# Retention attention and a dropless mixture of experts in one kernel: where the routing, the loads and the scaling stand in the attention steps

## The chip, the cores and the metric

The kernel runs on one core of a Trainium2 chip, in one launch. The metric is the device time of the launch in microseconds. Before the change it is 497.69 us, the median of three runs (497.06 to 498.72).

## What is computed

Four sequences of 768 tokens with 8 heads of 64 go through a recurrent retention; the result, read as 3072 rows of 512 features, goes through a mixture of 8 experts in which each row takes its best expert and no row is dropped.

```python
for t in range(S):                                       # B, H, S, D = 4, 8, 768, 64
    state = gamma * state + k[:, :, t] outer v[:, :, t]
    y[:, :, t] = scale * q[:, :, t] @ state
x = y.transpose(0, 2, 1, 3).reshape(3072, 512)
logits = x @ w_gate                                      # 512 x 8
e = argmax(logits); gate_w = softmax(logits)[e]
out = gate_w * (relu(x @ w1[e]) @ w2[e])                 # w1: 8 x 512 x 1024, w2: 8 x 1024 x 512
```

All is in float32.

## The kernel before, in words

The attention is cut into 12 steps, `steps = [(m, b)]`: three blocks m of 256 tokens for each of the four sequences b. In a step the 256 tokens lie on 128 partitions as pairs (e = 0, 1). A recurrence over 256 tokens becomes matrix products: `scale_q` and `scale_k` (L388 to L400) multiply q and k by powers of gamma, with GpSimd for all steps but the first; `transpose` (L402) turns them on TensorE into PSUM tiles `tr`, and ScalarE copies them to `qT` and `kT`; `scores` (L433) multiplies kT with qT into PSUM tiles `sc`, and VectorE masks them into `am` (L445); `values` (L473) multiplies `am` with v into y; `products` (L448) forms k-v products `new`, which VectorE adds to the running state (L466, L468); `past` (L488) adds q times the old state to y, and copies y to `xTg`, two copies for y[1]; `to_rows` (L508) transposes it to rows `xg` on VectorE, and `store` (L516) writes a group of rows to DRAM as `x_d`.

A group c is 512 rows, those of two steps, and is ready behind the second of them. `place(c)` (L531) is its routing, a generator that is advanced in pieces: `parts` (products with w_gate) and the group's store; `lgp` (transposes), logits, argmax and gate, a chain of small VectorE operations; `rk` (ranks of rows within their expert) and another chain (`seen` to `at`); the piece from `told` to `here`; and `found`, a product that puts row numbers into an inverse list `inv`. In group 3 (`FIRST`) the head of that list, `src_e`, then starts four early gathers of rows of the first expert from `x_d`, by GpSimd's indirect DMAs, into `xs2`.

The order on PE, ScalarE, GpSimd, VectorE and the DMA queue SP is the order in which the program writes the instructions (`manual_schedule`); each engine takes its instructions in turn and waits for semaphores. Before the change a step s reads: values(s), products(s), load(s+3), scaling of s+2, scores(s+1), past(s), one piece of routing, two `to_rows`, transpose(s+2), one piece of routing. Groups are chained: the next one's pieces begin where the last one's end. After step 11 the early rows are brought into order (`early_rows`, VectorE copies to `xe`, PE transposes `tre`), and the expert layers begin: `layer1` (L218, `hp`) for 256 early rows of expert 0, `pair` (L266, `yp`, a seven-product scheme for layer 2), then for every expert `layer1` and `layer2` (`ye`).

PSUM has 8 buffers here, four with the tag "sc" (for `sc`, `new`, `rk`, `found`, `hp`) and four with "ty" (for `y`, `tr`, `parts`, `lgp`, `tre`, `yp`, `ye`). A tile takes the buffer that was given up longest ago, and its first matmul waits for the last reader of the tile before.

Of the kernel before, what the change touches and what calls it, by code (L numbers as in the profile page):

```python
# [13 lines left out]
F32 = mybir.dt.float32  # L14
# [4 lines left out]
ALU = mybir.AluOpType  # L19
AX = mybir.AxisListType  # L20

P = 128


NC = 6
# [16 lines left out]
def inner(ap, n):  # L42

    dims = [list(d) for d in ap.ap]
    return bass.AP(tensor=ap.tensor, offset=ap.offset, ap=dims + [[0, n]])


def middle(ap, n):

    dims = [list(d) for d in ap.ap]  # L50
    return bass.AP(tensor=ap.tensor, offset=ap.offset, ap=[dims[0], [0, n]] + dims[1:])
# [3 lines left out]
def kernel(  # L55
# [11 lines left out]
    nc = tc.nc  # L67
    B, H, S, D = q.shape
# [3 lines left out]
    HP = H // 2  # L72
    NT = N // P
    DT = DM // P
# [14 lines left out]
    def ps(tag, bufs, name):  # L89
        return psum.tile([P, 512], F32, tag=tag, name=name, bufs=bufs)  # L90

    L = 32
    Q = P // L
# [226 lines left out]
    HALF = EARLY // P  # L320
# [26 lines left out]
    with ExitStack() as actx:  # L347
# [29 lines left out]
        def load(s):  # L377

            m, b = steps[s]
            got = {}  # L380
            for nm, src in (("k", k), ("q", q), ("v", v)) if s else (("q", q), ("k", k), ("v", v)):
                got[nm] = att.tile([P, H, 2 * D], F32, tag=nm, name=nm, bufs=2 if nm == "q" else 3)
                for hs in ([ts(i, HP) for i in range(2)] if s == 0 else [slice(0, H)]):
                    nc.sync.dma_start(got[nm][:, hs, :], src[b, hs, ts(m, 2 * P), :].rearrange(
                        "h (t e) d -> t h (e d)", e=2))
            qkv[s] = got

        def scale(s, nm, kept, base, bufs, muls):  # L388
            m, b = steps[s]
            kept[s] = att.tile([P, 2, H, D], F32, tag=f"{nm}s", name=f"{nm}s", bufs=bufs)  # L390
            for hs in ([ts(i, HP) for i in range(2)] if s == 0 and nm == "q" else [slice(0, H)]):
                for e in range(2):
                    muls[e].tensor_tensor(out=kept[s][:, e, hs, :], in0=qkv[s][nm][:, hs, ts(e, D)],  # L393
                                          in1=inner(dec[:, ts(base + 2 * m + e, H)][:, hs], D), op=ALU.mult)

        def scale_q(s, muls=[nc.gpsimd] * 2):
            scale(s, "q", qss, 0, 2, muls)

        def scale_k(s, muls=[nc.gpsimd] * 2):
            scale(s, "k", kss, NC, 3, muls)  # L400

        def transpose(s):  # L402


            of = {"q": qss.pop(s), "k": kss[s]}
            kT = att.tile([P, HP, 2, P], F32, tag="kT", name="kT", bufs=1)
            qT = att.tile([P, HP, P, 2], F32, tag="qT", name="qT")

            def turned(nm, es, pieces=1):
                trs = [ps("ty", 4, "tr").rearrange("p (a t) -> p a t", a=HP) for _ in es]  # L410
                for i in range(pieces):
                    for e, tr in zip(es, trs):
                        for a in range(i * HP // pieces, (i + 1) * HP // pieces):
                            nc.tensor.transpose(
                                tr[:, a, :], of[nm][:, e, 2 * a : 2 * a + 2, :].rearrange("p h d -> p (h d)"), ident)
                return trs

            def q_turned():
                for e, tr in enumerate(turned("q", range(2), 2) if s == 0 else [turned("q", [e])[0] for e in range(2)]):
                    (nc.vector.tensor_copy if e and s == 0 else nc.scalar.copy)(qT[:, :, :, e], tr)  # L420

            if s == 0:
                q_turned()
            for e in range(2):
                nc.scalar.copy(out=kT[:, :, e, :], in_=turned("k", [e])[0])  # L425
            if s:
                q_turned()
            front[s] = (kT, qT)
# [102 lines left out]
        def place(c):  # L531
# [14 lines left out]
            for b in range(B):  # L546
                nc.tensor.transpose(tr[:, b, :], lgT[:, ts(b, P)], ident)  # L547
            lg = att.tile([P, B, E], F32, tag="lg", name="lg")
# [26 lines left out]
            nc.tensor.matmul(rk, lhsT=ones_b, rhs=middle(acc[:, c, :], B), start=False, stop=True)  # L575
            seen = att.tile([P, E], F32, tag="seen", name="seen")
# [17 lines left out]
            if c < NC - 1:  # L594
                yield
# [32 lines left out]
        AHEAD = 3  # L628
# [3 lines left out]
        scale_q(0, [nc.vector] * 2)  # L632
        scale_k(0, [nc.gpsimd, nc.vector])
        transpose(0)
        nc.sync.dma_start(wg[:, :, 0:E], w_gate.rearrange("(dt p) e -> p dt e", p=P))
        scale_q(1)
        scale_k(1)
# [3 lines left out]
        xe = keep.tile([P, HALF, DM], F32, tag="xe", name="xe")  # L641

        def early_rows():
            for t in range(HALF):
                nc.vector.tensor_copy(xe[:, t, :].rearrange("p (a q l) -> p q a l", q=Q, l=L),
                                      xs2[0][:, t, :].rearrange("p (q a l) -> p q a l", q=Q, l=L))
                tr = ps("ty", 4, "tre").rearrange("p (a t) -> p a t", a=DT)
                for dt in range(DT):
                    nc.tensor.transpose(tr[:, dt, :], xe[:, t, ts(dt, P)], ident)
                if t:  # L650
                    nc.scalar.copy(out=xTa[:, :, ts(t, P)], in_=tr)
                else:
                    nc.vector.tensor_copy(xTa[:, :, ts(t, P)], tr)

        rest = iter(())
        step = lambda: next(rest, None)
        scores(0)
        for s in range(END):
            y = values(s)
            products(s)  # L660
            if s + AHEAD < END:
                load(s + AHEAD)
            if s + 2 < END:
                scale_q(s + 2)
                scale_k(s + 2)
            if s == 0:
                transpose(1)
            if s + 1 < END:
                scores(s + 1)
            else:  # L670
                early_rows()
            past(s, y)
            step()
            for i in range(2):
                to_rows(2 * s + i)
            if s + 2 < END:
                transpose(s + 2)
            if s in (2, 3):
                nc.gpsimd.memset(xs2[s % 2], 0.0)
            step()  # L680
            if s == END - AHEAD:
                wa = [weights1(first, 0)]
            if s == END - 2:
                wa.append(weights2(first, 0))
            if s % 2:
                rest = chain(rest, place(s // 2))
# [4 lines left out]
        he = [t[:, i, :] for t in [att.tile([P, 2, FH * P], F32, tag="k", name="he", bufs=3) for _ in range(2)]  # L691
              for i in range(2)]
        me = att.tile([P, 4, DH], F32, tag="v", name="me", bufs=3)
# [4 lines left out]
        for f in range(FT):  # L698
            layer1(EARLY, xTa, wa[0], hTa, f)
            if f in (0, 1, 2, 4):  # L700
                step()
            if f == 3:
                ne = count()
# [198 lines left out]
```

## Time and profile before

| what | us |
|---|---|
| median of the runs (lowest, highest) | 497.69 (497.06, 498.72) |
| the profiled execution, its own time | 496.23 |
| its span, first to last instruction | 494.4 |
| first `values` of step 0 | 13.59 |
| first `values` of step 11, the last | 130.46 |
| first `hp` of the early rows | 143.33 |
| first `yp` of the early rows | 166.27 |
| first `hp` of the second expert | 194.01 |
| busy: PE, VectorE, GpSimd, ScalarE | 459.4, 273.8, 136.9, 111.8 |

In the profile PE is TensorE's matmuls, PEld its weight loads, DVE VectorE, ACT ScalarE, POOL GpSimd, SP the DMA queue of SyncE. A row of a timeline has the start, the length, engine, line, operation, output and inputs, how many instructions were merged, and in brackets the idle time of that engine just before and what ended it. A row of the waits has the engine and line that waited, what it waited for, the total in us, how often, and the longest. The granted clock is a share of TensorE's full clock.

### The profile page before, as it was taken

The numbers are of one execution on the slowest core, as the hardware profiler recorded it, in microseconds if no ns is written. First come the engines' busy times: TensorE is split into PE (matmuls) and PEld (weight loads), VectorE is DVE, ScalarE is ACT, GpSimd is POOL, SyncE is SP. The second block draws the span as 40 slices with busy tenths as digits, with TensorE's granted clock in tenths as the row PEclk, the third lists the DMA queues.
The fourth block names the chain that finished last, engine by engine and source line by source line (L and its number), as shares of the span: only waits on it lengthen the run. The fifth ranks groups of instructions, "written<-read, shape, count | busy, mean of one in ns | idle before, by whom it ended". The sixth has DMA issues, their size and how long they took to land.

```text
span 494.4 us, 10414 instructions
## 1 busy us (share of the span) xinstructions
PE 459.4 (93%) x4350; PEld 324.6 (66%) x4350; DVE 273.8 (55%) x550; ACT 111.8 (23%) x231; POOL 136.9 (28%) x135
## 2 busy tenths in 40 slices
PE   7899699969869999999999999999999999999993
PEld 4788587848646894555667547668656865855782
DVE  3446878787657887095815361654654339271320
ACT  3254235415211110121120221123112111112110
POOL 3674624330300632306013301601601240200111
PEclk8999999989958999999999999999999999999998
DMA  9977677972913139907004800750650290150011
GB/s 241 282 208 220 175 190 191 261 235 80 266 64 85 42 132 335 346 3 244 20 27 114 330 1 28 239 217 19 225 219 5 70 376 36 43 191 1 27 43 46
DMA packets 68594, 72.64 MB, mean 147 GB/s; under 512 B 3978, under 2 KB 53130, under 8 KB 68496
## 3 DMA queue, kind: packets, MB, share of 16 engines
q1 hardware_dynamic: 63232, 58.74, 38.8%
q0 software_dynamic: 5120, 12.60, 7.2%
q8 instruction: 55, 0.90, 0.8%
q14 instruction: 43, 0.35, 0.2%
q10 hardware_dynamic: 144, 0.05, 0.0%
HBM read 60.88 MB, written 14.68 MB: 153 GB/s over the span
## 4 chain that ended last, share of the span: by engine, by line
PE 65%; DVE 3%; issue 1%; POOLq 0%; ACT 0%; DVEq 0%
PE hp L221 33%; PE yp L274 19%; PE ye L234 12%; DVE xT L209 2%; PE parts L539 0%; DVE two_e L189 0%; PE found L617 0%; POOLq L898 0%; DVE he L252 0%; DVE he L251 0%; DVE xs L280 0%; PE lgp L547 0%; ACT hTa L223 0%; DVE at L188 0%; DVE far_e L194 0%
## 5 line engine op out<-in xcount | busy, mean ns | idle before, releaser
L221 PE MATMUL hp<-xTs,w1t 128*128 128x392 f32 (+5 forms) x384 | 127.5, 493 | 0.5 <-issue 0.5
L221 PEld LDWEIGHTS hp<-xTs,w1t 128*128 128x128 f32 x384 | 72.9, 190 | 53.3 <-issue 30.9
L309 POOL DMA_INDIRECT out_dram<-o,dst x30 | 33.0, 1100 | 227.2 <-ACT o L242 135.7
L209 DVE STREAM_TRANSPOSE xTs<-xs 32x512 f32<-32x512 f32 x96 | 67.5, 703 | 50.7 <-DMA xs<-x_d,src 49.4
L234 PE MATMUL ye<-w2t,hT 128*8 128x128 f32 (+7 forms) x496 | 66.4, 360 | 0.0
L223 ACT ACTIVATE hT<-hp 128x392 f32<-128x392 f32 (+6 forms) x64 | 29.6, 468 | 147.0 <-PE hp L221 133.4
L234 PEld LDWEIGHTS ye<-w2t,hT 128*8 128x8 f32 (+7 forms) x496 | 32.7, 123 | 31.3 <-issue 28.7
L166 POOL DMA_INDIRECT xs<-x_d,src x28 | 38.3, 1369 | 36.4 <-DVE gate_e L201 28.2
L442 PE MATMUL sc<-qT,kT 64*64 64x128 f32 x768 | 30.1, 289 | 9.0 <-DVE state L468 6.9
L280 DVE SCALAR_TENSOR_TENSOR u<-yp,gate,m 128x256 f32<-128x256 f32 x14 | 6.8, 484 | 56.8 <-PE yp L274 51.5
L393 POOL TENSOR_TENSOR qs<-q,dec 128x512 f32<-128x512 f32 x22 | 22.5, 1044 | 47.0 <-DMA q<-in_q_dram 19.2
L445 DVE TENSOR_TENSOR am<-sc,causal 128x512 f32<-128x512 f32 x48 | 30.2, 684 | 9.2 <-PE sc L442 9.2
L442 PEld LDWEIGHTS sc<-qT,kT 64*64 64x64 f32 x768 | 24.9, 143 | 12.2 <-DVE state L468 9.2
L274 PE MATMUL yp<-ws,hs 128*128 128x256 f32 x144 | 32.1, 379 | 0.0
L483 PE MATMUL y<-am,v 64*64 64x128 f32 x768 | 29.9, 274 | 1.9 <-issue 0.8
L274 PEld LDWEIGHTS yp<-ws,hs 128*128 128x128 f32 x144 | 27.3, 190 | 3.8
L483 PEld LDWEIGHTS y<-am,v 64*64 64x64 f32 x768 | 23.5, 133 | 7.4 <-ACT kT L425 3.4
L274 PE MATMUL yp<-w2t,hT 128*128 128x256 f32 x112 | 26.6, 380 | 0.0
L393 POOL TENSOR_TENSOR ks<-k,dec 128x512 f32<-128x512 f32 x23 | 24.6, 1091 | 3.9 <-DMA k<-in_k_dram 3.9
L274 PEld LDWEIGHTS yp<-w2t,hT 128*128 128x128 f32 x112 | 21.2, 190 | 5.4 <-issue 2.8
L221 PE MATMUL hp<-xTa,w1t 128*128 128x256 f32 (+1 forms) x128 | 24.5, 349 | 0.0
L221 PEld LDWEIGHTS hp<-xTa,w1t 128*128 128x128 f32 x128 | 20.6, 204 | 3.7 <-issue 1.7
(189 smaller groups left out, 543.2 us busy)
## 6 DMA issues: line engine op xcount, KB each, us to landing
w1t<-in_moe_w_dram SPq DMA_DIRECT2D x8, 2048.0 KB, 13.8
w2t<-in_moe_w_dram SPq DMA_DIRECT2D x8, 2048.0 KB
x_d<-xg SPq DMA_DIRECT2D x24, 256.0 KB, 5.0
k<-in_k_dram SPq DMA_DIRECT2D x11, 512.0 KB, 7.2
q<-in_q_dram SPq DMA_DIRECT2D x11, 512.0 KB, 7.7
v<-in_v_dram SPq DMA_DIRECT2D x11, 512.0 KB, 5.6
q<-in_q_dram SPq DMA_DIRECT2D x2, 256.0 KB, 3.2
k<-in_k_dram SPq DMA_DIRECT2D x2, 256.0 KB, 4.6
```

Of the source, the lines that this page charges most:

```text
L166: nc.gpsimd.indirect_dma_start(out=xs[:, t, :], out_offset=None, in_=x_d[0:rows, :], in_offset=bass.IndirectOffsetOnAxis(ap=idx[:, t : t + ...
L209: nc.vector.transpose(xT[ts(g, L), :, 0 : n * P].rearrange("p a (t r i) -> p r t a i", r=Q, i=L)[:, r, :, :, :], xs[ts(r, L), tiles[0] : t ...
L221: nc.tensor.matmul(hp, lhsT=w1t[:, 0, dt, ts(f, P)], rhs=xT[:, dt, 0:n], start=(dt == 0), stop=(dt == DT - 1))
L223: nc.scalar.activation(out=hT[:, f, 0:n], in_=hp, func=AF.Relu)
L234: nc.tensor.matmul(y[j * z : j * z + m, 0:c], lhsT=hT[:, f, t * P + r0 : t * P + r0 + m], rhs=w2t[:, 0, f, ts(j, c)], start=(f == 0), stop ...
L274: nc.tensor.matmul(y, lhsT=a[:, f, :], rhs=b[:, f, :], start=start and f == 0, stop=f == FH - 1, skip_group_check=True)
L280: nc.vector.scalar_tensor_tensor(out=to, in0=y, scalar=g[i], in1=plus, op0=ALU.mult, op1=ALU.add)
L309: done = nc.gpsimd.indirect_dma_start(out=out[:, :], out_offset=bass.IndirectOffsetOnAxis(ap=idx[:, t : t + 1], axis=0), in_=o[:, t, :], i ...
L393: muls[e].tensor_tensor(out=kept[s][:, e, hs, :], in0=qkv[s][nm][:, hs, ts(e, D)], in1=inner(dec[:, ts(base + 2 * m + e, H)][:, hs], D), o ...
L442: nc.tensor.matmul(sc[j][ts(half, C), a, :], lhsT=kT[ts(j, D), a, e, ts(half, C)], rhs=queries(s, a, j, half), start=True, stop=True)
L445: nc.vector.tensor_tensor(out=am[e][j], in0=sc[j], in1=middle(causal[:, e, :], HP), op=ALU.mult)
L483: nc.tensor.matmul(y[half][ts(j ^ half, D), a, :], lhsT=vt[r, 2 * a + j, ts(e, D)], rhs=am[e][j][r, a, :], start=(a == 0 and e == 0), stop ...
```

## The change

Seven things are moved or altered.

1. `place` yields at three further places, so that it has seven pieces for every group: behind `lgp`, behind `rk`, and behind `at` for the last group too. A plan, `plan`, names where each piece of groups 0 to 4 is issued. For n = 2c + 1 it is: `parts` and the store at the end of step n ("B"); `lgp` and its chain behind products of step n+1 ("D"); `rk` behind past of n+1 ("A"); the rank chain behind its `to_rows` ("T"); `told` to `here` behind products of n+2 ("D"); `found` behind its past ("A"). For group 4 `found`, and for group 5 everything, come between the early rows' `layer1` calls.
2. `load` is four steps ahead, not three; k has two buffers, not three, and v four, not three.
3. In the first step q and k are loaded, scaled (on VectorE alone) and transposed in halves of the heads, q and k in turn.
4. Every step is transposed as q and k of the first half of the heads, then of the second; a PSUM tile holds both e of two head pairs.
5. The scaling of step s+3 (before: s+2) is issued behind scores(s+1). GpSimd first copies one column of the first `am` of step s+1 to `turn_of`, so that it can't start sooner.
6. `xs2` is set to zero ahead of the first step, not in steps 2 and 3.
7. The early rows are ordered into `xe` by GpSimd at the end of step 10, not by VectorE behind step 11. The first expert's w1 is asked for at the end of step 8 (before: 9), its w2 at that of 9 (before: 10).

```diff
         def load(s):
             m, b = steps[s]
-            got = {}
-            for nm, src in (("k", k), ("q", q), ("v", v)) if s else (("q", q), ("k", k), ("v", v)):
-                got[nm] = att.tile([P, H, 2 * D], F32, tag=nm, name=nm, bufs=2 if nm == "q" else 3)
-                for hs in ([ts(i, HP) for i in range(2)] if s == 0 else [slice(0, H)]):
+            got = {nm: att.tile([P, H, 2 * D], F32, tag=nm, name=nm, bufs=bufs)
+                   for nm, bufs in (("k", 2), ("q", 2), ("v", 4))}
+            halves = [ts(i, HP) for i in range(2)]
+            for nm, hs in ([(nm, hs) for hs in halves for nm in "qk"] + [("v", slice(0, H))]) if s == 0 else [
+                    (nm, slice(0, H)) for nm in "kqv"]:
...
+        def scale(s):
+            m, b = steps[s]
+            qss[s] = att.tile([P, 2, H, D], F32, tag="qs", name="qs")
+            kss[s] = att.tile([P, 2, H, D], F32, tag="ks", name="ks", bufs=3)
+            for hs in [ts(i, HP) for i in range(2)] if s == 0 else [slice(0, H)]:
+                for nm, kept, base in (("q", qss, 0), ("k", kss, NC)):
+                    for e in range(2):
+                        (nc.gpsimd if s else nc.vector).tensor_tensor(
...
         def transpose(s):
...
+            for i in range(2):
+                for nm in "qk":
+                    tr = ps("ty", 4, "tr").rearrange("p (e a t) -> p e a t", e=2, a=2)
+                    for e in range(2):
+                        for a in range(2):
...
+                    put = nc.vector.tensor_copy if (s, i, nm) == (0, 1, "k") else nc.scalar.copy
+                    put(turned[nm][:, :, ts(i, 2), :], tr)
...
-        AHEAD = 3
+        AHEAD = 4
...
+        scale(0)
         transpose(0)
...
+        scale(1)
+        scale(2)
+        for t in xs2:
+            nc.gpsimd.memset(t, 0.0)
...
-        rest = iter(())
-        step = lambda: next(rest, None)
+        placing = [place(c) for c in range(NC)]
+        plan = {}
+        for c in range(NC - 1):
+            n = 2 * c + 1
+            for at, pieces in ((n, "B"), 1), ((n + 1, "D"), 2), ((n + 1, "A"), 1), ((n + 1, "T"), 1), ((n + 2, "D"), 1), (
+                    (n + 2, "A"), 1):
+                plan.setdefault(at, []).extend([c] * pieces)
...
         for s in range(END):
             y = values(s)
             products(s)
+            step(s, "D")
             if s + AHEAD < END:
                 load(s + AHEAD)
-            if s + 2 < END:
-                scale_q(s + 2)
-                scale_k(s + 2)
             if s == 0:
                 transpose(1)
             if s + 1 < END:
                 scores(s + 1)
             else:
-                early_rows()
+                for t in range(HALF):
...
+                        nc.tensor.transpose(tr[:, dt, :], xe[:, t, ts(dt, P)], ident)
+                    nc.scalar.copy(out=xTa[:, :, ts(t, P)], in_=tr)
+            if s + 3 < END:
+                nc.gpsimd.tensor_copy(turn_of, masked[s + 1][0][0][:, 0, 0:1])
+                scale(s + 3)
             past(s, y)
-            step()
+            if s + 1 < END:
+                step(s, "A")
             for i in range(2):
                 to_rows(2 * s + i)
+            step(s, "T")
             if s + 2 < END:
                 transpose(s + 2)
-            if s in (2, 3):
-                nc.gpsimd.memset(xs2[s % 2], 0.0)
-            step()
+            step(s, "B")
+            if s == END - 2:
+                for t in range(HALF):
+                    nc.gpsimd.tensor_copy(xe[:, t, :].rearrange("p (a q l) -> p q a l", q=Q, l=L),
+                                          xs2[0][:, t, :].rearrange("p (q a l) -> p q a l", q=Q, l=L))
             if s == END - AHEAD:
                 wa = [weights1(first, 0)]
-            if s == END - 2:
+            if s == END - 3:
                 wa.append(weights2(first, 0))
-            if s % 2:
-                rest = chain(rest, place(s // 2))
...
             layer1(EARLY, xTa, wa[0], hTa, f)
-            if f in (0, 1, 2, 4):
-                step()
+            advance(*{0: (NC - 2, NC - 1), 1: (NC - 1, NC - 1), 2: (NC - 1, NC - 1, NC - 1), 4: (NC - 1,)}.get(f, ()))
```

## The prediction, made before the changed kernel ran

> **What bounds the kernel now.** I read the chain that ended last first. It is TensorE (PE) from 194.01 us to the end (hp L221, ye L234, yp L274) with under 0.5 us of waits: from there the expert layers run at PE speed, and a change to the attention stage can only move them earlier. So the question is when the expert layers start. The windows cut at the first matmul of each step's `values` show where PE stands still before that. Columns: window, length, busy us of PE, PEld, DVE, ACT, POOL, granted clock, DMA share, GB/s.
>
> ```profile
> core 0: us, PE busy (x) PEld busy (x) DVE busy (x) ACT busy (x) POOL busy (x), PEclk, DMA share, GB/s
> ...
> 54.51:68.25 13.74, 10.46 (x258) 8.31 (x257) 11.91 (x23) 4.95 (x10) 4.09 (x4) 1.00 0.58 147
> 68.25:77.00 8.75, 8.36 (x247) 7.33 (x246) 7.12 (x25) 3.47 (x8) 4.05 (x4) 1.00 0.78 215
> ...
> 96.50:112.77 16.27, 11.62 (x225) 9.58 (x225) 13.06 (x22) 5.00 (x10) 6.51 (x6) 0.90 0.83 250
> ...
> 130.46:143.33 12.87, 8.63 (x142) 6.41 (x142) 3.79 (x15) 0.81 (x2) 3.16 (x4) 0.72 0.58 205
> 143.33:166.27 22.94, 20.43 (x96) 15.09 (x95) 18.74 (x71) 4.09 (x10) 2.94 (x3) 0.86 0.23 56
> ```
>
> Step 5 (68.25) is clean at 8.75. Steps 4 and 8 take 13.74 and 16.27. The last step and the first expert's early rows take 12.87 + 22.94, partly at a reduced clock. The list of waits over 13 to 145 us names the first cause:
>
> ```profile
> PE sc L442 <- DVE state L468: 6.9, 2, 3.9
> ```
>
> The second pair of `sc` tiles takes the PSUM buffers of `new`, which the state addition empties; that addition stands on DVE behind the routing piece told..here. DVE's timeline shows this piece clean (step 6), then in step 8:
>
> ```profile
> 79.52 0.74 DVE L612 TENSOR_SCALAR here<-rrow,prow 128x128 bf16<-128x128 bf16 x4
> 80.68 0.95 DVE L468 TENSOR_TENSOR state<-new,state 128x256 f32<-128x256 f32 x2 [0.43 <-PE new L460]
> ...
> 103.70 1.51 DVE L612 TENSOR_SCALAR here<-rrow,prow 128x128 bf16<-128x128 bf16 x4
> 105.13 0.41 DVE L468 TENSOR_TENSOR state<-new,state 128x256 f32<-128x256 f32 x1
> ```
>
> Clean, the piece runs 77.80 to 80.26 (2.46 us); in step 8 it runs 99.66 to 105.21 (5.55). GpSimd's timeline tells why, and when the early gathers start:
>
> ```profile
> 102.06 2.62 POOL L393 TENSOR_TENSOR ks<-k,dec 128x512 f32<-128x512 f32 x2
> 129.39 1.23 POOL L166 DMA_INDIRECT xs<-x_d,src_e  x1 [24.71 <-DVE src_e L180]
> ```
>
> The scaling (100.04 to 104.68) lies beside the slow piece. In step 4 it is the same (scaling 56.29 to 60.38, PE idle 3.02). PE's timeline gives the stalls; the last bracket is the idle time ahead:
>
> ```profile
> 105.60 1.76 PE L442 MATMUL sc<-qT,kT 64*64 64x128 f32 x27 [3.90 <-DVE state L468]
> ...
> 137.94 1.09 PE L649 MATMUL tre<-ident,xe 128*128 128x128 f32 x4 [1.84 <-DVE xe L645]
> 140.24 1.08 PE L649 MATMUL tre<-ident,xe 128*128 128x128 f32 x4 [1.21 <-DVE xe L645]
> ...
> 149.32 0.80 PE L617 MATMUL found<-val,here 128*128 128x160 bf16 x4 [2.51 <-DVE here L612]
> ```
>
> **What the Trainium skill says.** "SBUF — State Buffer", Who interferes with whom: DVE and GpSimd share a port pair as an exclusive lock, held for a whole instruction, and the second one waits. The trace agrees: L600 takes 0.98 at 101.15 beside the scaling and 0.17 at 78.57 without it. "TensorE: Matmul & The Clock Gate", What's actually happening: an idle window of some 3.4 us halves the clock and a busy one restores it. Agreed: behind the 3.90 wait the clock is 0.52 from 105.6 to 109; from 138 to 146 it is 0.50. "GPSIMD Engine Reference", Engine selection: one-input operations run at about line rate, two-input ones some 2x slower; used below for the `xe` copies, which GpSimd doesn't do in this trace.
>
> **The change, part by part.** V is the start of `values`, P the end of `past`. In clean steps the state addition starts V+3.0 to 3.7 (step 5: +3.24) and P is V+6.2 to 6.7 (step 5: +6.23). From P on, the two y copies on ACT take 1.8, then the first two transposed copies 0.55 each, and the next `values` needs both PSUM buffers: P+2.95. I use +3.2 and +6.3, and add 0.2 per step for PE's small unexplained gaps (0.2 to 0.7 each in steps 5 to 8).
>
> *First step in halves.* Scaling, turning and copying in halves lets `k` of the first half go while the second lands. The last half still lands at about 7.44 (today's DVE wait for k); then two DVE multiplies (0.38 each), 4 transposes (0.5), the four small DVE operations (0.6) and one copy (0.62) give kT at 9.5 against 11.0, and the first mask at 10.6 against 12.55. But step 2's scaling starts when q lands (18.79, same order of loads) and ends at 22.84; turning it takes 1.4 more, so V(1) is 24.3 against 26.06: **gain 1.8**.
>
> *Routing behind the state additions.* The scores' wait for state (3.02 + 3.90, with 0.70 of issue and some 1.6 of half clock behind it: 3.4 us at 0.52) goes. `parts` moves to the end of odd steps, `lgp` behind `products`, the told..here piece of a group a step earlier. What is late next is `am`, now behind the piece, and with it PE's `found` and `rk`, whose PSUM buffer is the one that the first `am` empties (4 "sc" buffers in turn). Odd step: addition 3.2 to 4.15, told..here 2.46 to 6.6, am to 7.25; `found` waits from P=6.3 to 7.3 (1.0), then 0.4, 16 transposes 2.1, `parts` 1.0: 10.8. Even step: `lgp` 0.53, routing chain 2.15 after the addition (6.4), first am 7.05, P=6.85, `rk` 7.2, then ACT's copies: 9.75. The last am is at 8.9 to 9.1, before the next V: the 2.2 to 2.5 us of DVE are hidden by past and the transposes; without that cover each piece would cost its whole length. Steps 1 to 10: 9.6, 9.3, 10.9, 9.7, 10.8, 9.7, 10.8, 9.2, 10.45, 7.9 (8 to 10 have one addition; 9 has the three pad operations; 10 has no transposes). Sum 98.35 + 10 x 0.2 = 100.35 against 104.40 (26.06 to 130.46): **gain 4.05**. Little, because clean steps get longer.
>
> *Scaling released by `turn_of`.* A 128x1 copy is not in the trace; the nearest rows (128x8 memset 0.09, iota 0.14) bound it at 0.1 to 0.3; I take 0.15. It can't gain by itself. Queued behind it on GpSimd are the four multiplies (4.1), and behind them the next loads of k and q on SP, which have two buffers. The multiplies run from V+7.4 to V+11.5, the next V+1.6 at the latest, clear of the piece that starts at V+4.2; they overlap the rank chain, which may stretch from 1.4 to 2.5 and still ends before the next addition. The first mask of the next step waits for `turn_of` in its turn: done long before.
>
> *Loads and stores.* SP: k(s+4) leaves at V+0.6 to 4.9 (behind the stores, 4.4 us of issue), lands 7 later (page: 7.2 and 7.7), needed at the next step's V+7: 4 us to spare. Cost 0; if landing took 5 more, see the rival.
>
> *The end.* The early gathers start a step earlier relative to the last step (`found` of group 3 in step 9, not 10), ahead of w2's 2 MB. On the times above src is ready at 114.3, the two gathers for `xs0` leave by 116.9 and land by 121.5 (4.5 to landing today); `tre` comes at 125.3. The two `xe` copies go to GpSimd: 0.43 (DVE's own) to 1.02 (its two-input multiply) each; behind all four gathers (5.2) either way done by 123.5. From V(11): products +2.85, told..here (now here) to +5.8, `tre` to +3.75, past to +4.85, hp f=0 to +6.6, found +7.0, y1 copies on DVE to +7.2, `parts` +8.25, f=1 +10.0, lgp +10.5, f=2 +12.2; DVE's transposes, `we` and inv push the routing chain to +12.9, so `rk` waits 0.7; f=3, f=4 to +16.55; found waits 0.8; f=5 to 7 end at **+23.1** at full clock. Today 35.81 (130.46 to 166.27). **Gain 12.7**: 3.05 of xe waits, 2.51 + some 5 of half clock, the rest gaps and order. Behind 166.27 nothing changes.
>
> **Sum.** 1.8 + 4.05 + 12.7 = 18.5. The profiled execution is 496.23 (span 494.4 + 1.8 around it) and becomes 477.7; the median shown is 497.69, 1.46 above it, so 479.2. I add 0.3 for `we`, which may find w2 just landing: **479.5**.
>
> **The rivals.**
> *A, as above: 0.62*, own range 475 to 484 (0.4 more or less per step, turn of the tail 2).
> *B, late transfers in the tail: 0.17.* Gathers took 8 us from issue to use at 129.39 behind a full DMA (share 0.94 to 0.99). If so again, `tre` waits 1 to 3 and the half clock stays for the early rows (5): 485 to 489. For it: DMA is full then. Against: w2 is issued behind the gathers.
> *C, better: 0.08.* If `found` doesn't wait and the steps keep 8.75 to 9.7, 5 to 6 less: 471 to 475.
> *D, slower: 0.10.* k and q, with two buffers, are loaded only after GpSimd's scaling; loop for two steps: 4.1 + stores 4.4 + issue 2.5 + landing 7.7 = 18.7, against 20.5 for the pair. If landings lengthen by over 4 us, the scaling slides 2.6 us, into the piece ahead of `am`: told..here takes 5.55, each pair some 5 us more, five pairs 25, less the 18.5: 504. The stalls of 19.2 us on GpSimd for q speak for it, the extra step of loads against it.
> *E, nothing: 0.03.* The time moves from `state` to `am` and the tail's gain is lost to B's causes: within 1.5 us of 497.7. 0.3% (1.5 us) is about what a measurement can tell.
>
> Range 473 to 489: A whole, most of B, half of C. Faster 0.87 (A, B, C), same 0.03, slower 0.10.
>
> **What would show it.** PE's wait for state gone; DVE's told..here near 2.46 everywhere with no scaling beside it; waits of about 1 us of `found` and `rk` for `am`; no `tre` wait for `xe`; clock 1.00 from 14 us on; first yp near 148. I am wrong if GpSimd waits for q or k behind `turn_of`, if `am` ends later than the next V, or if the clock stays halved around the first hp.

## The result, and the profile after

The changed kernel takes 479.6 us (median of four runs, 479.07 to 480.68), beside 498.21 for the kernel before on the same chip (the three runs named above and a fourth of 502.52): a ratio of 0.961, with a 95% interval of 0.955 to 0.968. A second series on another chip, beside the last experiments, gave 0.966 (0.961 to 0.971). The profiled execution is 479.07 us, with a span of 477.4. A ratio leaves out executions that lie over 1.5% above the kernel's fastest; for one kernel below (the second run with a whole first step) these are five of six, and no ratio is given.

| | before | after | gained |
|---|---|---|---|
| first `values` of step 1 | 26.06 | 24.14 | 1.92 |
| first `values` of step 11 | 130.46 | 125.43 | 5.03 |
| first `hp` of the early rows | 143.33 | 131.68 | 11.65 |
| first `yp` of the early rows | 166.27 | 149.15 | 17.12 |
| end of the profiled execution | 496.23 | 479.07 | 17.16 |

Everything is won ahead of the first `yp`. The windows of the changed kernel, cut at `values` of steps 4, 5 and 6, then for step 8, then at `values` of step 11, the first `hp` and the first `yp` (columns as in the prediction):

```profile
core 0: us, PE busy (x) PEld busy (x) DVE busy (x) ACT busy (x) POOL busy (x), PEclk, DMA share, GB/s
54.75:64.70 9.95, 8.74 (x253) 7.61 (x249) 6.39 (x20) 3.39 (x8) 4.43 (x7) 1.00 0.78 197
64.70:77.37 12.67, 10.33 (x252) 8.01 (x252) 8.71 (x28) 4.88 (x10) 4.32 (x6) 1.00 0.69 182
...
99.15:108.00 8.85, 8.56 (x222) 7.69 (x218) 5.55 (x18) 3.26 (x7) 3.62 (x6) 1.00 0.73 187
125.43:131.68 6.25, 5.93 (x140) 4.83 (x137) 5.74 (x20) 2.33 (x5) 0.18 (x1) 1.00 1.02 336
131.68:149.15 17.47, 17.00 (x94) 13.38 (x91) 16.11 (x58) 4.09 (x10) 2.93 (x3) 1.00 0.40 108
```

Step 4 fell from 13.74 to 9.95, step 8 from 16.27 to 8.85, and the two windows of the tail from 12.87 and 22.94 to 6.25 and 17.47, at full clock instead of 0.72 and 0.86. But step 5, clean before at 8.75, is now 12.67. VectorE's timeline of the changed kernel, the routing piece of steps 5 and 7 with the state addition:

```profile
69.87 0.95 DVE L456 TENSOR_TENSOR state<-new,state 128x256 f32<-128x256 f32 x2 [3.24 <-PE new L448]
70.74 0.16 DVE L589 CAST told<-gate 128x4 bf16<-128x4 f32 x1
...
72.49 0.74 DVE L601 TENSOR_SCALAR here<-rrow,prow 128x128 bf16<-128x128 bf16 x4
73.14 2.48 DVE L433 TENSOR_TENSOR am<-sc,causal 128x512 f32<-128x512 f32 x4
...
94.66 0.74 DVE L601 TENSOR_SCALAR here<-rrow,prow 128x128 bf16<-128x128 bf16 x4
```

The piece stands behind the addition and takes 2.5 us in both steps (70.74 to 73.23 in the first). On GpSimd's timeline the scaling starts only behind `turn_of`, and the `xe` copies lie behind the gathers:

```profile
73.89 0.18 POOL L668 COPY turn_of<-am 128x1 f32<-128x1 f32 x1 [8.36 <-DVE am L433]
74.03 2.05 POOL L396 TENSOR_TENSOR qs<-q,dec 128x512 f32<-128x512 f32 x2
76.04 2.04 POOL L396 TENSOR_TENSOR ks<-k,dec 128x512 f32<-128x512 f32 x2
...
118.23 1.25 POOL L166 DMA_INDIRECT xs<-x_d,src_e  x1 [8.57 <-DVE src_e L180]
...
123.41 0.62 POOL L681 COPY xe<-xs 128x512 f32<-128x512 f32 x1
125.00 0.61 POOL L681 COPY xe<-xs 128x512 f32<-128x512 f32 x1 [0.98 <-DMA xs<-x_d,src_e]
```

PE's timeline shows what is late now:

```profile
69.09 0.75 PE L448 MATMUL new<-v,ks 64*64 64x64 f32 x36 [1.61 <-issue]
...
96.05 0.44 PE L606 MATMUL found<-val,here 128*128 128x160 bf16 x4 [1.04 <-DVE am L433]
...
129.62 1.09 PE L664 MATMUL tre<-ident,xe 128*128 128x128 f32 x8
...
133.51 0.44 PE L606 MATMUL found<-val,here 128*128 128x160 bf16 x4
...
139.57 0.19 PE L560 MATMUL rk<-ohs,before 128*128 128x32 bf16 x1 [0.28 <-DVE ohs L552]
```

The waits for `state` and `xe` are gone; `found` waits for the first mask in one step only. Most of what is left is "issue": PE stands still with no wait that the profile shows, 2.58 us ahead of 30.74, 1.61 ahead of 69.09, 1.52 ahead of 91.39, and 8.6 us in eight gaps before step 11. These gaps are the second subject of the experiments.

### The profile page after: what moved, and what is told of

Read it like the earlier page. It is cut to its first block, busy times and chain, and to the rows that moved or that the text cites. A ratio compares the mean times of both kernels' runs of the same rounds, so it can differ in the third digit from the quotient of the medians.

```text
span 477.4 us, 10419 instructions
## 1 busy us (share of the span) xinstructions
PE 450.1 (94%) x4350; PEld 318.0 (67%) x4350; DVE 263.0 (55%) x550; ACT 112.2 (24%) x232; POOL 136.9 (29%) x145
## 4 chain that ended last, share of the span: by engine, by line
PE 65%; DVE 4%; issue 1%; POOLq 0%; ACT 0%; DVEq 0%
PE hp L221 33%; PE yp L274 20%; PE ye L234 12%; DVE xT L209 2%; DVE two_e L189 0%; DVE we L263 0%; POOLq L897 0%; DVE he L252 0%; DVE he L251 0%; PE found L606 0%; DVE xs L280 0%; ACT hTa L223 0%; DVE inv L609 0%; DVE lg L538 0%; DVE dl L542 0%
## 5 line engine op out<-in xcount | busy, mean ns | idle before, releaser
L430 PE MATMUL sc<-qT,kT 64*64 64x128 f32 x768 | 26.2, 273 | 3.6 <-issue 3.2
L471 PE MATMUL y<-am,v 64*64 64x128 f32 x768 | 27.7, 273 | 1.0 <-DVE am L433 0.8
L471 PEld LDWEIGHTS y<-am,v 64*64 64x64 f32 x768 | 22.4, 133 | 9.0 <-ACT qT L415 4.3
L430 PEld LDWEIGHTS sc<-qT,kT 64*64 64x64 f32 x768 | 21.9, 133 | 6.4 <-issue 5.3
L396 POOL TENSOR_TENSOR ks<-k,dec 128x512 f32<-128x512 f32 x22 | 22.5, 1043 | 0.0
L221 PE MATMUL hp<-xTa,w1t 128*128 128x256 f32 (+1 forms) x128 | 22.4, 330 | 0.0
L221 PE MATMUL hp<-xT,w1t 128*128 128x392 f32 x64 | 21.3, 493 | 0.9 <-DVE at L188 0.9
```

Of the source, the lines that this page charges most:

```text
L221: nc.tensor.matmul(hp, lhsT=w1t[:, 0, dt, ts(f, P)], rhs=xT[:, dt, 0:n], start=(dt == 0), stop=(dt == DT - 1))
L396: (nc.gpsimd if s else nc.vector).tensor_tensor(out=kept[s][:, e, hs, :], in0=qkv[s][nm][:, hs, ts(e, D)], in1=inner(dec[:, ts(base + 2 * ...
L430: nc.tensor.matmul(sc[j][ts(half, C), a, :], lhsT=kT[ts(j, D), a, e, ts(half, C)], rhs=queries(s, a, j, half), start=True, stop=True)
L471: nc.tensor.matmul(y[half][ts(j ^ half, D), a, :], lhsT=vt[r, 2 * a + j, ts(e, D)], rhs=am[e][j][r, a, :], start=(a == 0 and e == 0), stop ...
```

## The experiments

The theories. *Collision* says that the slow routing piece came from GpSimd's scaling beside it, so that the gate, the copy to `turn_of`, is what counts, and the place of the piece on VectorE little. *Place* (the prediction's own wording) says that putting the piece behind the state addition wins the steps, and that the gate wins nothing by itself. For the tail, the earlier gathers stand against the earlier routing; for the gaps of PE, the bytes of the loads against the moment at which they start.

All runs in one table. V(n) is the first `values` of step n; "gaps" is PE's idle time with "issue" between 13 and 140 us. V, yp and gaps come from the one profiled execution of each kernel; with the old places, the whole first step (both runs) and q first it was the longest of its series, so V(11), yp and gaps of these four rows may be high.

| kernel | ratio to before (95%) | V(1) | V(11) | yp | gaps |
|---|---|---|---|---|---|
| before | 1 | 26.06 | 130.46 | 166.27 | 4.6 |
| changed | 0.961 (0.955 to 0.968) | 24.14 | 125.43 | 149.15 | 8.6 |
| changed, again | 0.966 (0.961 to 0.971) | 24.46 | 124.95 | 148.80 | 6.9 |
| told..here ahead of the addition | 0.965 (0.957 to 0.972) | 24.16 | 124.86 | 149.38 | 6.3 |
| no `turn_of` | 0.971 (0.963 to 0.979) | 24.56 | 129.81 | 154.42 | 5.8 |
| both | 0.990 (0.982 to 0.998) | 24.04 | 138.79 | 164.82 | 6.3 |
| before, with the plan alone | 1.006 (1.003 to 1.008) | 26.77 | 144.09 | 173.38 | 2.8 |
| early gathers a step later | 0.969 (0.959 to 0.978) | 24.24 | 129.50 | 158.68 | 11.9 |
| no loads from step 2 on | not compared | 24.08 | 123.38 | 146.53 | 3.4 |
| changed, routing at the old places | 0.977 (0.970 to 0.984) | 24.26 | 133.59 | 165.91 | 16.2 |
| first step whole | 0.969 (0.962 to 0.976) | 26.45 | 138.89 | 162.04 | 14.5 |
| first step whole, again | none | 26.28 | 133.09 | 156.81 | 13.2 |
| q asked for first | 0.961 (0.957 to 0.966) | 22.95 | 130.20 | 153.91 | 10.9 |
| q first, rk and found later | 0.958 (0.953 to 0.964) | 23.49 | 123.42 | 148.44 | 8.0 |

**Gate and place.** Four kernels: the changed one, and it with one or both of these undone. The first puts told..here at the end of step n+1, ahead of the state addition again:

```diff
-((n + 1, "T"), 1), ((n + 2, "D"), 1), (
+((n + 1, "T"), 1), ((n + 1, "B"), 1), (
```

> The changed kernel with one edit: the routing piece told..here stands ahead of the state addition again (at the end of the even step, behind the rank chain), while GpSimd's scaling keeps its place. Theory 1 (the old stall was a collision: piece and scaling at the same time, 5.5 us for 2.46): the piece stays near 2.5, the state addition comes at most 1.3 late, found waits less for am; time 478.5 to 481.5 against 479.6. Theory 2 (the place ahead of the addition is what costs): the wait of scores for state is back with 3 us or more in each odd step, 4 x 3 = 12, so 488 to 492.

The second takes the gate away:

```diff
-                nc.gpsimd.tensor_copy(turn_of, masked[s + 1][0][0][:, 0, 0:1])
```

> The changed kernel without the copy to turn_of: GpSimd scales as soon as its data and buffers allow; pieces stay behind the state addition. Theory 1: the scaling drifts to where q lands or a buffer comes free, in some steps beside told..here or the gate chain; each hit makes a piece 2 to 3 longer, am later than the next values by up to 1 to 2, so 480 to 486. Theory 2 (place alone): no effect, 479 to 480.5.

The third has both edits:

> The changed kernel with both edits: told..here ahead of the state addition, and no turn_of. Theory 1: where the scaling falls on the piece the old stall is back, 3 to 4 us with some half clock behind it, in two or three of the odd steps: 485 to 493, clearly more than the sum of the two edits alone. Theory 2: the same as with the piece ahead alone, 488 to 492 for both.

Measured: 481.19 us (479.5 to 483.08), 485.01 (483.17 to 487.08) and 494.49 (491.6 to 496.45), beside 499.3 for the kernel before on that chip. The third lies above the 485 to 493 that were expected of a collision. With the gate, the place doesn't show: 0.965 against 0.961 and 0.966. Without it, the place is worth 9.5 us. The gate itself is worth 13.3 us with the piece ahead of the addition (494.49 less 481.19), and behind it 2.6 to 4.8 (the ratio of 0.971 less the changed kernel's two, times 499.3; these intervals overlap, so the trace has to carry it). The list of PE's waits in the kernel without the gate, 13 to 160 us (total, times, longest):

```profile
PE found L606 <- DVE am L433: 5.6, 3, 3.4
PE rk L560 <- DVE am L433: 3.8, 5, 1.4
```

In the changed kernel these two are 1.0 and 0.7. That is 7.7 us more of waits, and its gaps are 2.8 less: 4.9 in all, where V(11) came 4.4 later. In the timeline of VectorE, still without the gate:

```profile
49.53 0.84 DVE L589 CAST told<-gate 128x4 bf16<-128x4 f32 x1
50.41 0.95 DVE L592 TENSOR_TENSOR less<-gate,told 128x4 f32<-128x4 f32 x1
51.40 0.98 DVE L589 CAST told<-less 128x4 bf16<-128x4 f32 x1
52.41 0.95 DVE L592 TENSOR_TENSOR less<-less,told 128x4 f32<-128x4 f32 x1
53.40 0.18 DVE L589 CAST told<-less 128x4 bf16<-128x4 f32 x1
```

and of GpSimd:

```profile
49.30 2.04 POOL L396 TENSOR_TENSOR qs<-q,dec 128x512 f32<-128x512 f32 x2 [7.21 <-DMA q<-in_q_dram]
51.30 2.04 POOL L396 TENSOR_TENSOR ks<-k,dec 128x512 f32<-128x512 f32 x2
```

Casts and subtractions of 128x4 take 0.84 to 0.98 us, about the length of one of the four multiplies (1.02), until 53.34, when the last multiply ends; the next takes 0.18. This is the exclusive lock of the Trainium skill's "SBUF — State Buffer", Who interferes with whom, which the prediction cited; the price here is one GpSimd multiply for each small operation. Behind the addition the stretched piece delays `am`, and with it `found` and `rk`. With both edits it delays the addition too, and PE's timeline has the old wait back:

```profile
53.45 2.51 PE L430 MATMUL sc<-qT,kT 64*64 64x128 f32 x32 [4.50 <-DVE state L454]
```

Collision holds; place, as the prediction worded it, doesn't: it counts only where the gate is missing.

**The plan alone.** The kernel before with the three further yields and `plan`, and nothing else of the change:

```diff
...
             products(s)
+            step(s, "D")
...
             past(s, y)
-            step()
+            if s + 1 < END:
+                step(s, "A")
...
```

> The kernel before with the routing plan alone (seven pieces at their new places, so also the early gathers a step earlier); loads three ahead, scaling, first step, early rows by VectorE and the weights as before. Theory 1: the tail gains most of its 12 us through the gathers, less 1 to 3 for VectorE's copies and w2 in front of PE's early rows; the steps gain the state waits and lose where the ungated scaling meets the pieces: 483 to 490. Rival (loads and scaling are what made the gain): less than 5 us better than before, 493 to 498.

Measured: 503.45 us (20 runs, 497.4 to 507.68), 0.6% slower than before by the ratio, where 483 to 490 had been expected. PE's timeline:

```profile
60.08 0.69 PE L618 MATMUL found<-val,here 128*128 128x160 bf16 x4 [7.48 <-DVE am L445]
...
85.74 0.69 PE L618 MATMUL found<-val,here 128*128 128x160 bf16 x4 [3.73 <-DVE am L445]
...
112.53 0.69 PE L618 MATMUL found<-val,here 128*128 128x160 bf16 x4 [4.21 <-DVE am L445]
```

`found` waits 17.4 us in four steps. In step 3 `here` takes 3.19 us from 56.23 on, beside multiplies from 54.59 to 59.2; the changed kernel's takes 0.74. The wait for `state` (6.9 before) fell to 0.6, and `am` took its place, at more than twice the length: this is the place of the prediction's rival D, though what leads there is the ungated scaling, not a late load. All of the loss lies in the steps: V(11) comes 13.6 us later than before. The tail, from there to `yp`, takes 29.29 us for 35.81, so 6.5 of it is won back there. In the kernel before, without the gate, the routing's places lose more in the steps than they win in the tail.

**The changed kernel with the old places.** All of the change except the plan; each piece stands where the kernel before had it:

```diff
-            for at, pieces in ((n, "B"), 1), ((n + 1, "D"), 2), ((n + 1, "A"), 1), ((n + 1, "T"), 1), ((n + 2, "D"), 1), (
-                    (n + 2, "A"), 1):
+            for at, pieces in ((n + 1, "A"), 1), ((n + 1, "B"), 2), ((n + 2, "A"), 2), ((n + 2, "B"), 1), ((n + 3, "A"), 1):
...
-            if s + 1 < END:
-                step(s, "A")
+            step(s, "A")
```

> The changed kernel with the routing pieces at the places of before (parts behind past of the second next step, told..here ahead of the state addition, found of group 3 in step 10); loads, turn_of, halves and the xe copies stay. Theory 1: without the collision the old places cost the steps little (told..here 2.5 to 3, waits for state under 1 each), so step 11 begins at 124 to 128, but the gathers are a step later and tre waits as with the late gathers: 484 to 492. Rival (place decides): the state waits of 3 and 4 us are back, and with the late gathers 494 to 500.

Measured: 490.77 us (488.23 to 495.04). No wait for `state` is left in the steps, and `here` takes 0.73 to 0.74 in all of them: with the scaling gated, the collision is gone there without the plan. What the old places cost is the tail, 32.3 us from V(11) to `yp` against 23.7. PE's timeline there:

```profile
149.06 0.80 PE L606 MATMUL found<-val,here 128*128 128x160 bf16 x4 [4.05 <-DVE here L601]
149.79 1.94 PE L527 MATMUL parts<-xTg,wg 128*32 128x512 f32 x8
```

Group 4's chain is a step later, `found` waits 4.05 for it, and `parts` runs at half speed behind that (1.94 against 1.06 in the changed kernel's tail). Of the 8.6 us that the tail loses, 3.2 fall ahead of the first `hp` (9.45 for 6.25), in short stops of PE with no wait shown and a clock of 0.82; what causes these isn't known. `tre` waits for nothing here, though the gathers are late. V(11) is also 8.2 later, but the gaps of this execution are 16.2 against 8.6, so that this part can't be given to the places; 124 to 128 had been expected for it, and 133.59 came.

**The gathers.** `found` of group 3, and with it the four early gathers, a step later, in step 10:

```diff
-                    (n + 2, "A"), 1):
+                    (n + 2 + (c == FIRST), "A"), 1):
```

> The changed kernel with one edit: found of group 3, and with it the early gathers, is issued behind past of step 10, not 9. Theory 1 (most of the tail's 12.7 is the gathers' step): they leave some 9 later, now behind w2's load, xe is ready some 12 later, PE stands 6 to 8 ahead of tre and the clock halves for part of the early rows: 486 to 491. Rival (the tail gained by order and by GpSimd's copies, the gathers had slack): 479.5 to 482.

Measured: 488.48 us (483.44 to 493.64). From V(11) to `yp` it takes 29.18, 5.5 more than in the changed kernel. PE's timeline, then the windows from that wait to the first `hp` and to the first `yp`:

```profile
137.61 1.97 PE L664 MATMUL tre<-ident,xe 128*128 128x128 f32 x8 [4.01 <-POOL xe L681]
```

```profile
core 0: us, PE busy (x) PEld busy (x) DVE busy (x) ACT busy (x) POOL busy (x), PEclk, DMA share, GB/s
...
137.61:141.43 3.82, 3.82 (x41) 3.16 (x41) 2.67 (x11) 1.17 (x2) 0.50 (x1) 0.50 0.27 87
141.43:158.68 17.25, 17.25 (x94) 13.60 (x91) 15.32 (x53) 4.09 (x10) 2.94 (x3) 0.98 0.31 75
```

The wait of 4.01 and the clock of 0.50 behind it account for the difference: of 3.82 us at half clock an estimated 1.9 are lost, and 4.01 + 1.9 is 5.9, for 5.5. "TensorE: Matmul & The Clock Gate" of the skill, What's actually happening, fits again. The tail's gain needs the gathers a step ahead.

**No loads.** From step 2 on no q, k and v are loaded; the data of steps 0 and 1 are used again. So the rows and the numbers of rows per expert are others, and behind the first `yp` this kernel takes 326.6 us against 329.9: its total isn't compared, only its steps.

```diff
...
+            if s > 1:
+                qkv[s] = dict(kept2[s % 2])
+                return
...
+            kept2[s] = got
```

> The changed kernel without the loads of q, k and v from step 2 on; the steps reuse the data of steps 0 and 1, so the result is another. Theory 1 for PE's gaps that no wait explains (8.6 us from 24 to 118 us, each while the DMA share is near 1): PE's instructions come late behind the loads; without them the gaps fall under 2 and, with steps 1 and 2 no longer bound by their loads, the time is 468 to 473. Rival (the gaps belong to PE's instruction stream whatever DMA does): gaps stay, 477 to 479.

Measured: 473.19 us (472.97 to 473.93). Steps 1 to 9 take 87.85 us, against 94.46 in the changed kernel. The gaps in them are 1.6 us, against 8.6. And `found` now waits in four steps, as the prediction had it. PE's timeline:

```profile
49.09 0.44 PE L611 MATMUL found<-val,here 128*128 128x160 bf16 x4 [0.89 <-DVE am L438]
...
69.22 0.44 PE L611 MATMUL found<-val,here 128*128 128x160 bf16 x4 [0.82 <-DVE am L438]
...
89.50 0.44 PE L611 MATMUL found<-val,here 128*128 128x160 bf16 x4 [1.04 <-DVE am L438]
```

The gaps come with the loads, and where they fall they hide the waits for `am`. (Its step 10 is 11.45 long, for 6.83, at a clock of 0.85 and with five stops of 0.3 to 0.4 us. The first run of the next kernel shows the like, 11.63. What causes that isn't known.)

**The first step in halves.** Step 0's q and k loaded and scaled whole, run in two series:

```diff
-            for nm, hs in ([(nm, hs) for hs in halves for nm in "qk"] + [("v", slice(0, H))]) if s == 0 else [
+            for nm, hs in [(nm, slice(0, H)) for nm in "qkv"] if s == 0 else [
...
-            for hs in [ts(i, HP) for i in range(2)] if s == 0 else [slice(0, H)]:
+            for hs in [slice(0, H)]:
```

> The changed kernel with the first step in whole tensors: q, k and v in one load each, each scaled whole by VectorE. My sum: the first values start about 2 later, but step 1 is bound by the scaling of step 2 (its q), so the end is 0.5 to 1.8 later: 480 to 481.5. Rival (PE takes every microsecond of the start on to the end): 2 or more, 481.6 or above.

> The changed kernel with q and k of step 0 loaded and scaled in whole tensors (its second run, beside the changed kernel). Theory 1 (the prediction's step: halves bring the second step's values 1.8 us forward): the first values of step 1 are 1.8 to 2.3 later, all steps move by it, total 481.4 to 482. Rival (halves only shift work; the first steps wait for the transfers of later steps anyway): step 2 makes the loss good and the total stays within 0.7 us of the changed kernel.

Measured: 486.43 us (484.57 to 493.88), then 485.75 beside 480.99 for the changed kernel. V(1) is 26.28 against 24.46: 1.82 later, as theory 1 says, and step 2 doesn't make it good. The total moves by 4.8, not 1.8, and V(2) by 5.5, in an execution whose gaps are 6.3 longer (13.2 against 6.9). Yet the sixth run of this kernel took 475.94, less than any run of the changed one. So 1.8 us is what halves bring to V(1), and what they bring to the total lies under the scatter of the executions and isn't settled; neither forecast of the total (481.4 to 482, or within 0.7 of the changed kernel) was met.

**q first.** From step 1 on, `load` asks for q, k, v:

```diff
-                    (nm, slice(0, H)) for nm in "kqv"]:
+                    (nm, slice(0, H)) for nm in "qkv"]:
```

> From step 1 on, load asks for q, k, v and not k, q, v. Theory 1 (PE's unexplained gaps, 8.6 us in all, come from transfers that arrive in a burst, since k and q leave together when GpSimd has ended both scalings): q's buffer is free 2 us before k's, so the transfers leave apart; at the start q of step 1 lands first and its scaling begins up to 2 us sooner. Gaps fall to 4 to 6 us, step 1's values come 1 to 2 us sooner, total 476 to 478.5. Rival (the gaps follow the bytes, not their spacing): gaps stay at 8 to 9, only the start gains, 478 to 479.6.

and with it `rk` and `found` behind the transposes:

```diff
-            for at, pieces in ((n, "B"), 1), ((n + 1, "D"), 2), ((n + 1, "A"), 1), ((n + 1, "T"), 1), ((n + 2, "D"), 1), (
-                    (n + 2, "A"), 1):
+            for at, pieces in ((n, "B"), 1), ((n + 1, "D"), 2), ((n + 1, "B"), 2), ((n + 2, "D"), 1), ((n + 2, "B"), 1):
...
-            step(s, "B")
+            if s + 1 < END:
+                step(s, "B")
```

> q first as in the run before it, and rk and found of each group issued behind the next transposes instead of behind past, so that PE doesn't stand before them until the first masks are done. Theory 1 (the waits of found and rk for am, 3.0 us in the run without loads, are on the path): they go, total 0.5 to 2 below the run before it, 474.5 to 478. Rival (the transposes then come sooner, but wait for ScalarE and the next step's values for the same copies, and found and rk come later to the state addition): no change or up to 2 slower, 478 to 480.5.

> The changed kernel again, beside the next three on one chip. 479.6, as before, ratio to the kernel before 0.961; it is the yardstick for the others.

Measured: the changed kernel 480.99 us (479.2 to 486.56), q first 479.83 (478.62 to 484.26), both 479.38 (475.3 to 482.73). q first brings V(1) 1.5 forward, but its gaps are 10.9 in the profiled execution (484.26, its longest), and its total doesn't fall to the 476 to 478.5 expected, so nothing supports the theory that spacing shrinks them. With both, `found` and `rk` no longer wait for `am`, but the tail gives 1.2 back (25.02 from V(11) to `yp` against 23.85), in a wait of `rk` that the list of PE's waits shows:

```profile
PE rk L560 <- DVE ohs L552: 1.6, 1, 1.6
```

Its ratio is the lowest of the kernels that do the whole work, 0.958, but the intervals of all three overlap: no version here is shown to beat the changed kernel.

## Why the prediction was right, and where its steps were not

*Halves, 1.8.* Right: 1.92 from the profiles, 1.82 with the halves undone, and by the way that was worked out: step 2's scaling starts at 18.71, for 18.79.

*Steps 1 to 10, 100.35.* Measured 101.29, a gain of 3.11 for 4.05. The sum is near by errors that offset each other. "I add 0.2 per step for PE's small unexplained gaps", 2.0 in all, was taken from steps 5 to 8 of the kernel before; the gaps are 8.6, which is 6.6 more. `found` was to wait 1.0 in each of the four odd steps that have it (3, 5, 7 and 9); it waited 1.04 once, 3.0 less, since a gap ahead of it lets VectorE catch up. Step 10 came 1.1 under its 7.9, and the other 1.6 or so, spread over the steps, isn't traced. Odd steps took 57.5 for 53.6 (7.5 of gaps among them), even ones 43.8 for 46.8. Without loads, where the gaps are 1.6, steps 1 to 9 are 9.4, 8.6, 10.1, 9.7, 10.5, 9.8, 10.5, 8.8, 10.5, each within 0.8 of the lengths worked out (without the 0.2), and `found` waits in all four.

*"It can't gain by itself."* This, on `turn_of`, is the step that was wrong. It was costed as a copy, 0.15 (measured 0.18), and its gain was put down to the places: the working assumed 2.46 us for told..here in every step, while without the gate single steps show 5.5. The plan alone costs 0.6%; the gate is worth 13.3 us with the piece ahead of the addition. A forecast of the plan by the same working would have had the wrong sign, and of the gate none at all.

*Loads, cost 0.* k and q arrive in time: from the first `turn_of` at 26.19 us on, GpSimd's scaling waits for nothing but `turn_of` and its mask. Rival D's trigger isn't there, while its mechanism, a slow piece ahead of `am`, is real wherever the gate is missing. But the loads cost PE's gaps, which this step didn't consider.

*The tail, +23.1.* Measured +23.72, a gain of 12.1 for 12.7. `hp` came at +6.25 for +6.6, `rk` waited 0.28 for 0.7, the `xe` copies take 0.62 and 0.61 (bounds 0.43 and 1.02), and the clock is 1.00. The runs show both causes: with late gathers 5.5 is lost, in a wait of `tre`; with the old places, late gathers among them, 8.6, of which at least the wait of `found` (4.05) is the routing's. Rival B didn't occur.

*The sum.* 17.16 less in the profiled execution, for 18.5. It lies 0.5 below the median of its runs where the one before lay 1.46 below; that made up 0.9 of the 1.3 missing, and the 0.3 for `we` most of the rest, so that a forecast within 0.1 us is partly luck.

## What to carry to other kernels

Where two engines block each other, price each moved piece with what runs beside it at its new place, and look for an edit that keeps the two apart: here the gate, 0.18 us long, did in the steps what the moved pieces could not, and the moves paid in the tail. Edits of this sort don't add: undo them singly and together. Where PE idles with no wait shown, look at where in the instruction stream the gaps stand, and at when the packets of the "instruction" queue end, before blaming a neighbour.

## What was not expected of the hardware

PE's "issue" gaps stand at fixed counts of instructions, not at fixed times or tiles. The number of matmuls before each gap of 0.5 us or more behind 24 us and before the tail (counted up the timeline; gap in us):

| kernel | matmuls before the gap (gap) |
|---|---|
| before | 984 (1.57), 2132 (0.70) |
| changed | 474 (2.58), 984 (0.60), 1239 (0.87), 1366 (1.61), 1494 (0.54), 1877 (1.52), 2388 (0.61) |
| changed, again | 474 (0.88), 729 (0.87), 984 (1.71), 1366 (1.06), 1494 (1.62) |
| no `turn_of` | 474 (2.11), 1494 (1.38), 1877 (1.21), 2388 (0.52) |
| q first | 474 (2.02), 984 (1.71), 1239 (0.86), 1366 (1.88), 1877 (2.89), 2388 (1.09) |
| q first, rk and found later | 474 (1.69), 983 (0.87), 1238 (0.85), 1493 (3.14), 2004 (1.41) |
| no loads | 1240 (0.50), 1752 (0.56), 2392 (0.54) |

The distances are 127 or 128 matmuls, or a multiple: 255, 510, 127, 128, 383, 511. Counted with the weight loads and the waits and branches that the trace lists for PE, every gap of 0.5 us or more in the fourteen traces stands at the same place of a block of 256 instructions, to within one. Which borders show a gap changes from run to run; the borders don't. The page of the changed kernel lists the DMA queues (packets, MB, share of the 16 engines' time):

```profile
q1 hardware_dynamic: 63216, 58.74, 40.3%
...
q8 instruction: 55, 0.90, 0.8%
```

A queue of kind "instruction" brings 0.90 MB in 55 packets of 16 KB; the page counts them on the same 16 engines as the loads. The windows of the changed kernel show how full these are in four of the gaps (the last column but one):

```profile
27.80:30.60 2.80, 0.36 (x9) 0.12 (x2) 0.52 (x2) 0.00 (x0) 2.58 (x3) 1.00 0.86 228
...
67.40:69.10 1.70, 0.09 (x6) 0.00 (x1) 0.00 (x0) 0.00 (x0) 0.00 (x0) 1.00 1.07 302
...
89.80:91.40 1.60, 0.07 (x7) 0.01 (x2) 0.00 (x0) 0.00 (x0) 0.00 (x0) 1.00 0.96 276
112.70:113.30 0.60, 0.03 (x2) 0.00 (x0) 0.53 (x3) 0.00 (x0) 0.00 (x0) 1.00 0.10 41
```

The long gaps lie where the engines are full, and a gap of 0.6 stands where they are nearly idle; without loads none is over 0.56 before step 10. The trace also keeps when each packet of queue q8 starts and ends. Five borders of the changed kernel (times in us):

| matmuls before the border | PE passes the border before | packet starts | packet ends | PE goes on | gap |
|---|---|---|---|---|---|
| 474 | 25.01 | 28.07 | 29.24 | 30.74 | 2.58 |
| 1366 | 61.46 | 66.44 | 67.62 | 69.09 | 1.61 |
| 1621 | 73.38 | 74.50 | 75.94 | 79.58 | none |
| 1877 | 83.97 | 88.83 | 90.03 | 91.39 | 1.52 |
| 2388 | 108.74 | 111.07 | 112.03 | 113.33 | 0.61 |

All 72 gaps of 0.5 us or more between 13 and 145 us, in the fourteen traces together, end 1.2 to 1.7 us behind the end of such a packet. Where the packet ended over 1.75 us before PE passed the border (139 of 297 borders), no gap of 0.3 us or more stands there. So PE goes on when a packet has come, and a gap is a packet that came late. The packet itself takes 0.9 to 2.0 us; what varies is its start. In the changed kernel it starts 1.1 to 1.2 us behind the border before where the DMA share in between is under 0.1 (three borders), and 4.9 and 5.0 where the share is about 1, ahead of the gaps of 1.52 and 1.61; but at other borders with full engines it starts after 0.7. The gap of 0.61 fits in: its packet started with the engines still full, and they fell idle before PE went on.

That the gaps come with the loads is shown by the kernel without them, and that they end with the packets by all traces. That a packet holds the instructions which PE waits for is the likely reading: its contents aren't in the trace, and no run moved the borders. The scatter of the changed kernel (479.2 to 486.56 on one chip) would follow from where a load meets a border; that isn't shown.
